# Squares and scales of weight tiles one product later, and earlier sums in the last block

## The chip, the cores and the metric

The kernel runs on one core of a Trainium2 chip. The metric is the device time of one execution in microseconds (us). The kernel before took 1020.46 us (median of three runs, 1018.66 to 1020.50); the run that the profiler recorded took 1019.09 us.

## What is computed

Four blocks follow each other on x, a matrix of 2048 tokens by 640 channels: a spectral block A, a mixer block B, then A and B again with the same weights. The change touches only the two mixer blocks.

```python
def _B_ref(x, w1, b1, w2, b2):           # x: (1, 2048, 640)
    h = _layernorm(x, axis=-1)
    u = jnp.einsum("bsd,sf->bdf", h, w1) + b1        # w1: (2048, 1728)
    u = _gelu(u)
    y = jnp.einsum("bdf,fs->bds", u, w2) + b2        # w2: (1728, 2048)
    return y.transpose(0, 2, 1)
...
x = x + _A_ref(_layernorm(x), A_w_r, A_w_i)
x = x + _B_ref(_layernorm(x), B_w1, B_b1, B_w2, B_b2)
x = x + _A_ref(_layernorm(x), A_w_r, A_w_i)
x = x + _B_ref(_layernorm(x), B_w1, B_b1, B_w2, B_b2)
```

## The kernel before

**Numbers in two halves.** TensorE (PE) multiplies float16 numbers, so each float32 operand is scaled and split into a high and a low float16 part, and a product is three matmuls: high by high, high by low, low by high. For a weight tile the parts are called `wh` and `wl`. ScalarE (ACT) makes `wh`, VectorE (DVE) makes `wl` out of the raw tile and `wh`.

**The first mixer block (`b1st`, L910).** Its weights come as 30 tiles, numbered m: 0 to 13 are columns of w1, 14 to 29 are columns of w2. Each tile has one product on PE: from m = 2 on product m is 96 matmuls of 320 columns for w1 (16 steps j of 6 matmuls, L978), and 82 for w2. Products 0 to 13 give the rows of u; product 14 is the first that reads u, in the order of its rows 0 to 13. A tile goes through these steps:

- load: `wload` (L845) reads it in two halves (c = 0 and 1) into `raw`. There are three buffers, and tile m + 3 takes that of tile m, half by half. It is asked for at the start of product m (`ahead`, L943); its DMA starts when the last reader of that half is done, and that is the making of `wl` of tile m.
- scan: `scan1` (L203) squares and sums each half on ACT (tiles `junk`, `sq`).
- scale: `scale1` (L210) has three steps, each run by one call of `step`: a reduction on DVE (`sqb`), a matmul of one column on PE with a matrix of ones, and on DVE some eight tiny operations that end in the tile's scale `s`.
- split: `wsplit` (L857) makes `wh` and `wl` of each half. Their buffers are free when the product two before has ended.
- sums: for the pairs of tiles (3, 2), (5, 4), ... (13, 12), DVE forms four sums S1 to S4 of half tiles (`wsum`, L893), which ACT and DVE split (`wssplit`, L901, tile `sp`) and GpSimd's queue (POOL) stores in DRAM for the second mixer block. S1 reads both halves of the odd tile.

After each w1 product, ACT reads it from PSUM (`t`, `q`), and ACT and DVE work out the gelu (`q`, `uf`). Once the scales of all w1 tiles are known, `scale_u` (L265) fixes one scale `su` for u, and `usplit` (L961) makes `uh` and `ul` of every row on DVE, in the order of `SEQ` (rows 6, 13, 0, 7, 1, 8, ... 5, 12). Row 12 is the last: it comes out of product 13.

**What sets the order.** The loops L989 to L1056 and L1086 to L1142 say at which step of which product each operation is written. Most of `b1st` is not pinned, so the scheduler of the framework places an engine's instructions by its own estimate of when they can start, beginning from that written order. On the chip each engine runs its list strictly in the order that comes out, and what waits holds up all behind it.

**The last block (`b2nd`, L1160).** Everything is pinned to the written order. Its second half multiplies by w2 in 56 products (n, L1600) of seven row blocks of u. The row block that is finished last (`LATE`) is left out of products 0 to 3 and added to all four together during n = 3. `hi` and `lo` (L1231, L1238) make the two parts of a weight sum three and two products ahead, `form` (L1220) makes the sums on DVE, `xbias` adds a bias to the rows of x on ACT, and `evict` (L1542) adds a finished product to x; for the first two products that takes an ACT copy `m` first.

Of the kernel before, what the change touches and what calls it, by code (L numbers as in the profile page):

```python
# [20 lines left out]
NJ, NG, NFT = 16, 16, 14  # L21
# [45 lines left out]
class Layers:  # L67
# [842 lines left out]
    def b1st(self, li):  # L910
# [78 lines left out]
        for ft in range(NFT):  # L989
# [10 lines left out]
            for j in run:  # L1000
                if ft % 2 and ft < NFT - 2 and 11 <= j < 15:
                    self.wsum(ft + 2, ("S1", "S3", "S2", "S4")[j - 11])
                if ft > 1:
                    m = ft + 1 - ft % 2
                    d = SEQ[m - 1]
                    if ft < m and j == 7:
                        q = [self.st[0][:, t:t + 1] for t in (d, d + 7)]
                        V.tensor_tensor(self.s1p[:, d:d + 1], *q, op=ALU.min)
                    if j in ((9, 14) if ft < m else (1, 7)):
                        self.wssplit(m, {9: "S1", 14: "S2", 1: "S3", 7: "S4"}[j])  # L1010
# [10 lines left out]
                else:  # L1021
                    if ft == 2 and j in (4, 5):
                        step(3)
                    if ft == 2 and j in (5, 6):
                        self.scan1(4, (j - 5,))
                    if ft == 2 and j == 7:
                        step(4)
                    if j in ((6, 8) if ft == 2 else (2, 4)):
                        next(steps)
                    if ft == 2 and j in (10, 11) or ft > 2 and j in (4, 5):  # L1030
                        step(ft + 2)
                    if j == 8 and ft == NFT - 3:
                        self.scale_u()
                    if j in (11, 13):
                        self.scan1(ft + 3, (j // 2 - 5,))
                    if j == 15:
                        step(ft + 3)
                    if ft == NFT - 2 and j % 2 or ft == NFT - 1 and j % 3 == 0 and 0 < j < 13:
# [47 lines left out]
        for j in range(NJ):  # L1086
            wh, wl = self.w.pop(NFT + j)
            ahead(NFT + j, (wh, wl))
            m = NFT + j
# [21 lines left out]
            for i, (ft, a) in enumerate(order):  # L1111
# [4 lines left out]
                if i in (4, 8):  # L1116
                    next(steps, None)
                if i in (6, 7):
                    step(m + 2)
# [40 lines left out]
    def b2nd(self, li):  # L1160
# [439 lines left out]
        for n in range(NP2 + 1):  # L1600
# [6 lines left out]
            if n == 3:  # L1607
                for k in range(4):
                    product(k, [LATE], start=False)
            if n in (2, 4):  # L1610
                xbias(n // 2 - 1)
            for k in {0: (), 1: (), 2: (), 3: (), 4: (0, 1, 2, 3)}.get(n, (n - 1,)):
                evict(k)
                q = ops[N1 + k][0]
                left[q] -= 1
                if not left[q] and q + 3 < NQ:
                    xload(q + 3)
                    extra[n + 4].append(lam(xbias, q + 3))
            if n == 5:
                xbias(2)  # L1620
            if n > 2:
                hi(N1 + n + 3)
            if n > 3:
                lo(N1 + n + 2)
# [303 lines left out]
```

## Time and profile before

| | us |
|---|---|
| median of three runs (lowest, highest) | 1020.46 (1018.66, 1020.50) |
| the profiled execution | 1019.09 |
| its span, first to last instruction | 1017.3 |
| PE busy / DVE busy / ACT busy | 968.7 / 782.9 / 577.6 |
| first mixer block, w1 products | about 210 to 372 of the span |
| first mixer block, w2 products | about 372 to 565 |
| last block, w2 products | about 853 to the end |

Times inside the span count from its first instruction. The difference of 1.8 us between the execution and its span lies outside the instructions. In the rows of a timeline stand: start, duration, engine, line of the helper that issues it (L59), operation, the tile written and those read, shape, count, and in brackets how long the engine was idle before and on what. A matmul's duration is its latency; the pace of PE is seen from start to start, 0.136 us for 320 columns.

### The profile page before, as it was taken

What the parts mean: (1) busy time and instruction counts of PE and PEld (TensorE: products, weight loads), DVE (VectorE), ACT (ScalarE), POOL (GpSimd) and SP (SyncE); (2) the same over time, 40 slices, a digit from 0 to 9 for tenths busy, and PEclk for the clock granted to TensorE, in tenths of its full rate; (3) what the DMA queues carried; (4) which work ended last, traced back from release to release, by engine and by line L of the source; (5) the groups of instructions that cost most, each with busy time, mean ns of one, the idle gap of its engine ahead of it and who ended that gap; (6) DMA issues with size and microseconds to landing.
All of it is one profiled execution on the core that took longest, in us unless ns stands there. A gap on an engine that the chain in (4) does not pass through costs nothing.

```text
span 1017.3 us, 20999 instructions
## 1 busy us (share of the span) xinstructions
PE 968.7 (95%) x8235; PEld 719.4 (71%) x8235; DVE 782.9 (77%) x1493; ACT 577.6 (57%) x890; POOL 299.9 (29%) x502
## 2 busy tenths in 40 slices
PE   3879999999999999999999799999999999999998
PEld 2768767667777767777777588776777777677776
DVE  7978968997866894666666689789965547898885
ACT  4857658687666654555553367685643434544531
POOL 6937857512211211222222278575000000000000
PEclk9599999999999999999999899999999999999999
DMA  7865346656665556465423465375444446755411
GB/s 230 278 187 163 116 157 225 218 170 247 227 215 200 189 166 247 142 189 154 135 90 111 128 183 181 93 230 173 151 160 167 166 158 222 247 183 190 152 45 53
DMA packets 67259, 176.45 MB, mean 173 GB/s; under 512 B 7996, under 2 KB 15320, under 8 KB 67160
## 3 DMA queue, kind: packets, MB, share of 16 engines
q1 hardware_dynamic: 59384, 146.92, 45.0%
q0 software_dynamic: 7776, 28.20, 7.5%
q8 instruction: 64, 1.05, 0.4%
q14 instruction: 35, 0.29, 0.1%
HBM read 127.24 MB, written 47.84 MB: 172 GB/s over the span
## 4 chain that ended last, share of the span: by engine, by line
PE 41%; DVE 27%; issue 10%; ACT 9%; POOL 7%; DMA 6%; SPq 0%; POOLq 0%; ACTq 0%; DVEq 0%
PE ps L59 41%; DVE wl L59 5%; DVE f L59 3%; DVE st L59 3%; POOL eo L59 3%; DMA xt<-x 2%; DVE s1l L59 2%; ACT wh L59 2%; DVE xt L59 2%; DVE Yl L59 2%; DMA w1S<-sp 1%; POOL xt L59 1%; ACT z L59 1%; DMA raw<-w 1%; DVE hl L59 1%
## 5 line engine op out<-in xcount | busy, mean ns | idle before, releaser
L59 PEld LDWEIGHTS <-wh 128*128 128x128 f16 x2602 | 252.4, 98 | 100.2 <-issue 2.1
L59 PEld LDWEIGHTS <-wl 128*128 128x128 f16 x1610 | 157.6, 98 | 62.8 <-issue 1.1
L59 PE MATMUL ps<-ul,wh 128*128 128x320 f16 x448 | 133.0, 299 | 0.1
L59 PE MATMUL ps<-uh,wl 128*128 128x320 f16 x448 | 133.0, 299 | 0.0
L59 PE MATMUL ps<-uh,wh 128*128 128x320 f16 x416 | 124.3, 299 | 0.0
L59 PE MATMUL ps<-hl,wh 128*128 128x320 f16 x496 | 102.9, 300 | 0.9 <-DVE hl L59 0.8
L59 PEld LDWEIGHTS <-wo 128*128 128x128 f16 x756 | 73.9, 98 | 29.7 <-DVE wo L59 1.0
L59 DVE SCALAR_TENSOR_TENSOR wl<-raw,s,wh 128x896 f16<-128x896 f32 (+2 forms) x64 | 74.5, 1168 | 12.4 <-ACT wh L59 12.2
L59 ACT ACTIVATE junk<-raw 128x896 bf16<-128x896 f32 (+1 forms) x60 | 59.5, 992 | 39.2 <-DMA raw<-w 39.0
L59 POOL TENSOR_TENSOR r<-v,mh 128x1 f32<-128x1 f32 x64 | 36.3, 567 | 151.1 <-DVE nm L59 141.2
L59 PE MATMUL ps<-tDi,Yh 128*128 128x322 f16 x320 | 72.7, 305 | 0.2
L59 DVE TENSOR_TENSOR f<-eo 128x256 f32<-128x256 f32 (+1 forms) x124 | 39.0, 367 | 38.5 <-POOL eo L59 37.9
L59 ACT ACTIVATE wh<-raw,s 128x896 f16<-128x896 f32 (+2 forms) x68 | 67.2, 1010 | 1.6 <-DVE s L59 1.6
L59 POOL TENSOR_TENSOR xt<-xt,ec 128x320 f32<-128x320 f32 x64 | 52.3, 839 | 34.9 <-DVE xt L59 34.7
L59 ACT ACTIVATE z<-xt,nb,r 128x640 f32<-128x640 f32 x31 | 28.5, 919 | 57.0 <-POOL z L59 44.5
L59 PE MATMUL ps<-ph,tS 128*128 128x321 f16 (+2 forms) x288 | 58.6, 286 | 1.3 <-DVE tb L59 1.3
L59 DVE BATCH_NORM_STATS2 st<-xt 128x6 f32<-128x320 f32 x126 | 55.2, 480 | 6.0 <-DMA xt<-x 5.0
L59 PE MATMUL ps<-u,wo 128*128 128x320 f16 x420 | 59.0, 299 | 0.7 <-DVE wo L59 0.7
L59 PE MATMUL ps<-hha,wh 128*128 128x320 f16 x288 | 58.8, 302 | 0.0
L59 POOL TENSOR_TENSOR eo<-z 128x320 f32<-128x320 f32 x62 | 53.3, 880 | 17.1 <-ACT z L59 15.1
L59 PE MATMUL ps<-tDi,Yl 128*128 128x322 f16 x192 | 56.6, 303 | 1.5 <-DVE Yl L59 1.5
L59 PE MATMUL ps<-tM,f 128*128 128x128 f32 x160 | 36.9, 395 | 21.8 <-DVE f L59 21.7
(250 smaller groups left out, 2374.1 us busy)
## 6 DMA issues: line engine op xcount, KB each, us to landing
xt<-x SPq DMA_DIRECT2D x79, 320.0 KB
raw<-w SPq DMA_DIRECT2D x32, 512.0 KB
w<-w SPq DMA_DIRECT2D x48, 321.0 KB
x<-xt SPq DMA_DIRECT2D x47, 320.0 KB
raw<-w SPq DMA_DIRECT2D x32, 448.0 KB
raw<-w2z SPq DMA_DIRECT2D x32, 448.0 KB
w1S<-sp POOLq DMA_DIRECT2D x24, 512.0 KB, 3.2
out<-xt SPq DMA_DIRECT2D x15, 320.0 KB
```

The costliest lines, as they stand in the source:

```text
L59: i = f(*a, **k)
```

## The change

In the first mixer block, for tiles 5 to 15, the scan of tile m is written in product m - 2 at steps 1 and 3 and no longer in product m - 3 at steps 11 and 13; its reduction at step 6 of product m - 2 and no longer at step 15 of product m - 3; its matmul and its tiny operations at steps 10 and 11 and no longer at 4 and 5. The splits stay where they were. Product 2 and product 14 carry tiles over by other steps, so that the places fit together; `scale_u` and the first reduction of `s1p` follow by four steps and one.

In the last block, the first four products are evicted two and two (n = 3 and 4) and no longer all at n = 4, the bias of the second row of x comes one product earlier, and `lo` of sum 6 is made at n = 3 between the two pairs of evictions.

```diff
@@ b1st, w1 products
-                    if ft < m and j == 7:
+                    if ft < m and j == 8:
...
-                    if ft == 2 and j in (4, 5):
+                    if ft == 2 and j in (6, 7):
                         step(3)
...
-                    if j in ((6, 8) if ft == 2 else (2, 4)):
+                    if j in ((9, 11) if ft == 2 else (2, 4)):
                         next(steps)
-                    if ft == 2 and j in (10, 11) or ft > 2 and j in (4, 5):
+                    if ft > 2 and j in (1, 3):
+                        self.scan1(ft + 2, (j // 2,))
+                    if j in (10, 11) or ft > 2 and j == 6:
                         step(ft + 2)
-                    if j == 8 and ft == NFT - 3:
+                    if j == 12 and ft == NFT - 3:
                         self.scale_u()
-                    if j in (11, 13):
-                        self.scan1(ft + 3, (j // 2 - 5,))
-                    if j == 15:
-                        step(ft + 3)
@@ b1st, w2 products
-                if i in (6, 7):
+                if j == 0 and i in (1, 3):
+                    self.scan1(m + 2, (i // 2,))
+                if i in ((8, 12, 13) if j == 0 else (6, 7)):
                     step(m + 2)
@@ b2nd
-            if n in (2, 4):
-                xbias(n // 2 - 1)
-            for k in {0: (), 1: (), 2: (), 3: (), 4: (0, 1, 2, 3)}.get(n, (n - 1,)):
+            if n in (2, 3):
+                xbias(n - 2)
+            for k in {0: (), 1: (), 2: (), 3: (0, 1), 4: (2, 3)}.get(n, (n - 1,)):
                 evict(k)
...
-            if n > 3:
+            if n == 3:
+                lo(N1 + 6)
+            if n > 4:
                 lo(N1 + n + 2)
```

What the scheduler makes of it shows in the lists of the engines. DVE, around the reduction `sqb` of tile 15, before: it stands behind the splits of u's rows 6, 13, 0, 7, 1, 8 and 2.

```order
L59 SCALAR_TENSOR_TENSOR ul2_546_3346<-uf2_547_3363,su_130,uh2_546_3332 128x640
L59 TENSOR_SCALAR s1_73<-qi1_732_5108 128x1
L59 SCALAR_TENSOR_TENSOR sp_735_5186<-S2_720_5021,sp1_79,sp_735_5186 128x1024
L59 TENSOR_SCALAR s1_73<-s1_73 128x1
L59 TENSOR_REDUCE sqb1_737_5197<-sq_734_5161 128x1
L59 TENSOR_SCALAR uh9_546_3339<-uf9_547_3370,su_130 128x640
```

And now (`qt` is the squared sum of tile 13, `uf4` the gelu of product 10, `qm` the first operation of `scale_u`):

```order
L59 SCALAR_TENSOR_TENSOR uf4_547_3365<-q_704_4886,t_703_4885 128x640
L59 TENSOR_SCALAR qt_76<-ps714_4978 128x1
L59 TENSOR_REDUCE sqb1_745_5267<-sq_743_5227 128x1
L59 TENSOR_SCALAR qi1_716_4989<-qt_76 128x1
L59 TENSOR_REDUCE qm_5003<-qt_76 128x1
```

The reduction has moved 39 instructions up: ahead of `scale_u` and of every split of u.

ACT, between the splits of tiles 10 and 11, before (`junk_69,sq_702` is the scan of tile 13, `sp` the splits of S1, S2 and S3 of the pair 11, `wh_697` the split of tile 11, `t` and `q` the reading of product 9):

```order
L59 ACTIVATE junk_69,sq_702_4851<-raw_695_4757 128x1024
L59 ACTIVATE sp_701_4835<-S1_686_4706,sp1_79 128x1024
L59 ACTIVATE sp_703_4872<-S2_689_4724,sp1_79 128x1024
L59 ACTIVATE junk_69,sq_702_4851<-raw_696_4759 128x1024
L59 ACTIVATE sp_712_4912<-S3_688_4716,sp1_79 128x1024
L59 ACTIVATE wh_697_4765<-raw_665_4470,s0_72 128x1024
```

And now, the same operations:

```order
L59 ACTIVATE junk_69,sq_711_4911<-raw_693_4752 128x1024
L59 ACTIVATE junk_69,sq_711_4911<-raw_694_4754 128x1024
L59 ACTIVATE sp_699_4826<-S1_685_4699,sp1_79 128x1024
L59 ACTIVATE sp_702_4869<-S2_688_4722,sp1_79 128x1024
L59 ACTIVATE wh_695_4760<-raw_663_4465,s0_72 128x1024
L59 ACTIVATE t_690_4744<-ps675_4605,b1s_67,c0_74 128x640
```

Both halves of the scan of tile 13 still stand ahead of the split of tile 11, now also ahead of S1 and S2; S3 has gone behind the split. Between the splits of tiles 9 and 10 the list of ACT is as before: scan of tile 12, then the split of tile 10.

DVE in the last block, both kernels (`xt` is an eviction, `wo0_1566` and `wo0_1568` are `lo` of sum 6, `wo1_1571` that of sum 7, S1 to S4 are formed sums):

```order
 L59 TENSOR_TENSOR S1_1565_12010<-raw_1554_11933,raw_1555_11935 128x896
-L59 TENSOR_TENSOR S2_1567_12044<-S1_1565_12010,raw_1556_11937 128x896
 L59 SCALAR_TENSOR_TENSOR xt_1552_11927<-ps1563_11952,c1_75,xt_1552_11927 128x320
 L59 SCALAR_TENSOR_TENSOR xt_1553_11930<-ps1563_11952,c1_75,xt_1553_11930 128x320
+L59 SCALAR_TENSOR_TENSOR wo0_1568_12050<-S1_1565_12010,sp_77,wo0_1568_12050 128x896
+L59 TENSOR_TENSOR S2_1569_12053<-S1_1565_12010,raw_1556_11937 128x896
 L59 SCALAR_TENSOR_TENSOR xt_1552_11927<-ps1564_11989,c1_75,xt_1552_11927 128x320
 L59 SCALAR_TENSOR_TENSOR xt_1553_11930<-ps1564_11989,c1_75,xt_1553_11930 128x320
-L59 SCALAR_TENSOR_TENSOR wo0_1566_12042<-S1_1565_12010,sp_77,wo0_1566_12042 128x896
 L59 TENSOR_TENSOR S3_1572_12081<-raw_1556_11937,raw_1554_11933 128x896
```

`lo` of sum 6 now stands ahead of the second sum and of the last two evictions; `lo` of sum 7 follows eight operations after S1, as before.

## The prediction

> **What bounds the kernel now.** I read the page first, then PE's waits in the first mixer block, then the timelines around the longest.
>
> ```profile
> span 1017.3 us, 20999 instructions
> PE 968.7 (95%) x8235; PEld 719.4 (71%) x8235; DVE 782.9 (77%) x1493; ACT 577.6 (57%) x890; POOL 299.9 (29%) x502
> PE ps L59 <- DVE sqb L59: 2.9, 2, 2.3
> PE ps L59 <- DVE wl L59: 0.2, 1, 0.2
> ```
>
> PE is busy for 95%, and in the w1 products it waits for almost nothing but the squared sums, 2.9 us in two places. The longer one is that of tile 15, in product 13:
>
> ```profile
> 357.77 0.43 PE L59 MATMUL ps<-hha,wl 128*128 128x320 f16 x2
> 360.52 0.16 PE L59 MATMUL ps<-sqb,ones 128*128 128x1 bf16 x1 [2.32 <-DVE sqb L59]
> ```
>
> The one-column matmul starts 2.75 us after the pair at 357.77, which takes 0.27, so 2.5 us are lost. Behind it comes a stretch at half clock, which the busy times by windows show (its columns: stretch, length, then busy time and count of PE, PEld, DVE, ACT and POOL, then the granted clock):
>
> ```profile
> 361.30:364.70 3.40, 3.40 (x15) 1.95 (x14) 3.40 (x7) 2.11 (x4) 1.44 (x1) 0.52 0.42 166
> ```
>
> 3.4 us at a clock of 0.52 are 1.7 us more. So the wait is worth 4.2 us to PE. But PE has another wait behind it, in product 14, which reads u:
>
> ```profile
> 381.81 0.30 PE L59 MATMUL ps<-uh,wh 128*128 128x320 f16 x1
> 382.24 0.30 PE L59 MATMUL ps<-ul,wh 128*128 128x320 f16 x1
> ```
>
> 0.43 from start to start, 0.30 too long: here PE waits for `ul` of row 12, the last to be split. So this end is set by DVE, by 0.3 us, and not by the wait of 4.2. What DVE did from the last scale of w1 on:
>
> ```profile
> 343.07 0.15 DVE L59 TENSOR_SCALAR qt<-ps 128x1 f32<-128x1 f32 x1
> 343.25 0.15 DVE L59 TENSOR_SCALAR qi<-qt 128x1 int32<-128x1 int32 x1
> 347.44 1.00 DVE L59 TENSOR_SCALAR uh<-uf,su 128x640 f16<-128x640 f32 x2
> ...
> 360.24 0.14 DVE L59 TENSOR_REDUCE sqb<-sq 128x1 bf16<-128x2 f32 x1
> 374.40 0.14 DVE L59 TENSOR_SCALAR qi<-s 128x1 int32<-128x1 int32 x1
> 381.30 0.88 DVE L59 SCALAR_TENSOR_TENSOR ul<-uf,su,uh 128x640 f16<-128x640 f32 x1
> ```
>
> And the windows of the same stretch:
>
> ```profile
> 343.00:349.50 6.50, 6.50 (x51) 4.67 (x50) 6.40 (x25) 4.32 (x7) 1.97 (x2) 1.00 0.62 206
> 349.50:358.00 8.50, 8.50 (x65) 6.05 (x62) 8.50 (x12) 5.24 (x6) 1.66 (x3) 1.00 0.42 147
> 358.00:375.00 17.00, 14.68 (x98) 9.97 (x97) 16.76 (x35) 9.20 (x13) 2.82 (x6) 0.90 0.57 190
> ```
>
> DVE, the third busy number, works 31.7 of 32 us. The block's turn from w1 to w2 is a DVE queue without holes, from 343.25 to `ul` of row 12 at 382.18.
>
> **The change, part 1: the new wait.** The scan of tile 15 needs tile 15 loaded:
>
> ```profile
> 339.86 2.91 SPq L851 DMA_DIRECT2D raw<-w  x2
> 344.12 0.95 ACT L59 ACTIVATE junk<-raw 128x896 bf16<-128x896 f32 x1 [2.39 <-DMA raw<-w]
> 348.30 0.95 ACT L59 ACTIVATE junk<-raw 128x896 bf16<-128x896 f32 x1 [1.06 <-DMA raw<-w]
> 375.18 1.03 ACT L59 ACTIVATE wh<-raw,s 128x896 f16<-128x896 f32 x1
> ```
>
> Its halves are asked for as `wl` of tile 12 frees its buffers, at 339.86 and 342.44 (2.91 for both issues, of which each takes 0.33), and the second lands at 348.30, 8.4 us after the first was asked for. The scan ends 1.1 later, at 349.4. Before, the reduction stood far down DVE's list and ran at 360.24: the load cost nothing. Now it stands right behind `qt` of tile 13, ahead of `scale_u` and all splits of u, and DVE's list is strict: DVE stops at about 343 and waits for the load. Behind it stand the same 31.1 us of DVE work (343.25 to 374.40, the scale of tile 15), and behind that the last chain on ACT and DVE: `wh` of tile 15, reading product 13, gelu, split of row 12 (375.18 to 382.18, 7.0 us). So row 12 is ready at B + 38.1, B being the start of DVE's block, 343.25 before (with 0.8 of slack, since ACT waited for another load).
>
> **Where B falls.** It is 9.5 us after the first half of `wl` of tile 12, which before ended at 339.8. Whether this comes earlier is a matter of a loop: `wl` of tile m frees the buffer, the load of tile m + 3 follows, its scan stands in ACT's list ahead of the split of tile m + 1.
>
> ```profile
> 257.22 1.28 DVE L59 SCALAR_TENSOR_TENSOR wl<-raw,s,wh 128x1024 f16<-128x1024 f32 x1 [0.41 <-ACT wh L59]
> 272.42 1.28 DVE L59 SCALAR_TENSOR_TENSOR wl<-raw,s,wh 128x1024 f16<-128x1024 f32 x1
> 285.36 1.28 DVE L59 SCALAR_TENSOR_TENSOR wl<-raw,s,wh 128x1024 f16<-128x1024 f32 x1 [0.88 <-ACT wh L59]
> 295.03 1.06 ACT L59 ACTIVATE junk<-raw 128x1024 bf16<-128x1024 f32 x1 [0.78 <-DMA raw<-w]
> 300.21 1.28 DVE L59 SCALAR_TENSOR_TENSOR wl<-raw,s,wh 128x1024 f16<-128x1024 f32 x1
> 310.11 1.06 ACT L59 ACTIVATE junk<-raw 128x1024 bf16<-128x1024 f32 x1 [3.10 <-DMA raw<-w]
> 312.33 1.28 DVE L59 SCALAR_TENSOR_TENSOR wl<-raw,s,wh 128x1024 f16<-128x1024 f32 x1 [0.88 <-ACT wh L59]
> 327.85 1.28 DVE L59 SCALAR_TENSOR_TENSOR wl<-raw,s,wh 128x1024 f16<-128x1024 f32 x1
> 338.55 1.28 DVE L59 SCALAR_TENSOR_TENSOR wl<-raw,s,wh 128x1024 f16<-128x1024 f32 x1 [0.89 <-ACT wh L59]
> ```
>
> These are the first halves of tiles 6 to 12, with the second scans of tiles 11 and 12. From tile 7 to 9 are 27.8 us, from 9 to 11 27.6; two products on PE are 192 x 0.136 = 26.1. So the loop is slower than PE, and the splits fall behind.
>
> An odd leg now: the second half of the load lands 8.4 after `wl` (295.03 - 286.64). Then scan 1.05, S1's split on ACT 1.05, four DVE operations (S1, S2, two new sums) at 1.2, `wl` 1.3: 16.6 us, where before 14.9 (tile 9) and 15.5 (tile 11) were enough, because the S1 and S2 splits ran during the load. An even leg: the second half of `wl` follows the first by 2.0 and not by 3.1, as no sum stands between; the load lands some 7.7 after, not 8.6; the rest stays at 3.5 (310.11 to 313.61): 11.1, where before 12.1. So a pair takes 27.7 as before, and only the start helps:
>
> ```profile
> 230.31 1.15 ACT L59 ACTIVATE sp<-S,sp 128x1024 f16<-128x1024 f32 x1 [2.82 <-DMA w1S<-sp]
> 239.76 1.15 ACT L59 ACTIVATE sp<-S,sp 128x1024 f16<-128x1024 f32 x1 [3.52 <-issue]
> ```
>
> These two waits shrink, since S1 of pair 3 is now split one `wl` (1.2 us) earlier and S1 of pair 5 no longer stands behind a scan. I take 2.8 us of lead at tile 6 (255.7 for the end of `wl`), as an estimate from these rows: less 4.6 on the three odd legs 7, 9, 11, plus 3.6 on the even ones 8, 10, 12, gives a lead of **1.8 us** at tile 12. Its ends are -1 (the loads land no earlier on the even legs) and 4 (the odd legs cost nothing more). B is then 338.0 + 9.5 = 347.6 and row 12 is split at 385.7, 3.5 us later than before; by the ends of the lead, 1.4 to 6.4.
>
> In those sums the load counts with the 5.9 us that the row shows for the second half (342.44 to 348.30). The Trainium skill's page "DMA: Bandwidth & Descriptors", section "Anatomy of one DMA", has about 2.0 us plus the bytes at 436 GB/s; for 448 KB that is an estimate of 3.1 us. By that rule B would be 2.8 earlier and the loss 0.7 and not 3.5; the row differs, and it decides.
>
> **What goes.** The wait of tile 15's matmul goes: it now stands 36 matmuls (4.9 us) later, and its reduction runs at 347.6, ahead of its place at about 362. So do the 0.2 at `wl` of tile 11. Both lie ahead of row 12 and are given back waiting for it. The wait of tile 3, 0.54 us in the list of waits, stays: its matmul moves by one place, and the three sums ahead of its reduction remain. Tile 16's sum is needed long after it is there. Product 15's tile and all later loads had over 5 us to spare, and PE does not wait from there to 557; so what is lost at row 12 shows in the end.
>
> **Part 2, the last block.**
>
> ```profile
> 871.44 1.80 PE L59 MATMUL ps<-u,wo 128*128 128x320 f16 x12 [0.71 <-DVE wo L59]
> 867.71 0.55 DVE L59 SCALAR_TENSOR_TENSOR xt<-ps,c,xt 128x320 f32<-128x320 f32 x1 [1.89 <-ACT m L59]
> 870.24 1.14 DVE L59 SCALAR_TENSOR_TENSOR wo<-S,sp,wo 128x896 f16<-128x896 f32 x1
> 872.76 1.14 DVE L59 SCALAR_TENSOR_TENSOR wo<-S,sp,wo 128x896 f16<-128x896 f32 x1
> ```
>
> PE loses 0.9 us (1.01 from start to start) for `lo` of sum 6, ready at 871.38. Now it comes after two evictions and no longer after four and a sum: about 869.6, and the wait goes. But `lo` of sum 7, at 873.9 before, still has eight operations after S1 ahead of it, DVE waits no less for `m`, and it comes at 874.1. PE, now 0.9 earlier, needs it at 873.4 and gets it at about the time at which it used it before (874.3). So 0.0, between -0.9 (sum 7 is in time) and +0.4 (the lag of 0.2 to 0.4 shows at a later sum).
>
> **The sum.** 1019.09 + 3.5 + 0.0 = 1022.6 on the profiled execution. That execution lies 1.4 below the median of 1020.46, and 3.5 on the median is 1024.0; I take 1023.4, between the two.
>
> **The rivals.** *Faster (the intended way):* the odd legs do not lengthen, and the loop follows PE. The deciding point is a lead of 5.3 us at tile 12, `wl` before 334.5; then row 12 is ready before 382.2. At best PE gains all that it lost: 4.2 + 0.3 at row 12 + 0.2 at tile 11 + 0.9 = 5.6, which is 1014.9 on the median. For it: ACT no longer stands in two halves around the sums. Against it: every scan stands ahead of a split and behind a load, as before. With the clock, the rows show half pace after an idle stretch of 2.3 us; the Trainium skill's "TensorE: Matmul & The Clock Gate", section "What's actually happening", has it after an idle window of about 3.4 us, by which 2.5 and not 4.2 would go at tile 15. The row speaks against that; the limit would be 1016.6.
>
> *No change:* tile 15's second half lands faster, as that of tile 16 does:
>
> ```profile
> 354.97 2.72 SPq L851 DMA_DIRECT2D raw<-w  x2
> 361.18 0.95 ACT L59 ACTIVATE junk<-raw 128x896 bf16<-128x896 f32 x1 [1.80 <-DMA raw<-w]
> ```
>
> Its issue begins at 357.36, and it lands 3.8 later, not 5.9. Then B is 345.5 and the loss 1.4; on the median, 1021.9.
>
> *Slower still:* the loads gain nothing on even legs, a lead of -1, and PE, which waits for rows 4 and 5 as well, runs at half clock behind them: 3.5 + 2.8 + about 1 = 7.3, 1027 between the execution and the median.
>
> **How the numbers follow.** The forecast's mechanism 0.72 (its own range 1020.8 to 1026.5), faster 0.13, no change 0.10, slower still 0.05. About 0.2% (2 us) is what a measurement of this kernel can tell from no change. A fifth of the forecast's own weight lies within it, so: faster 0.14, same 0.20, slower 0.66. The range 1018.8 to 1026.8 leaves out the faster cases and the far end of the slow ones.
>
> **What would show it.** Right: a new DVE wait of 3 to 7 us ahead of `sqb`, ended by ACT's `junk`, at about 343 to 348; no PE wait for `sqb` in product 13; PE waiting for `ul` of rows 4, 5 and 12, the last at about 385.7; `wl` of tile 12 at 336 to 340; in the last block the wait for `wo` moved by one sum. Wrong: `wl` of tile 12 before 334.5, or DVE without that hole.

## The result and the profile after

The changed kernel takes 1028.05 us (median of four runs, 1027.96 to 1030.97), the kernel before, on the same chip, 1020.48 (1018.66 to 1021.68). The ratio is 1.0083 with a 95% interval of 1.0059 to 1.0106: slower by 7.6 us between the medians, more than twice what was forecast and beyond the range. The profiled execution took 1027.96 us.

First the page, its span and busy times; then the list of PE's waits, with the five rows that concern the two mixer blocks (us in all, times, longest):

```profile
span 1026.2 us, 20994 instructions
PE 972.6 (95%) x8235; PEld 722.0 (70%) x8235; DVE 781.7 (76%) x1493; ACT 577.8 (56%) x890; POOL 299.4 (29%) x502
```

```profile
PE ps L59 <- DVE wl L59: 4.4, 4, 2.6
PE ps L59 <- DVE uh L59: 2.6, 1, 2.6
PE ps L59 <- DVE ul L59: 1.5, 2, 1.0
PE ps L59 <- DVE wo L59: 0.4, 1, 0.4
PE ps L59 <- DVE sqb L59: 0.4, 1, 0.4
```

The span is 8.9 us longer. The wait for the squared sums has shrunk from 2.9 us to 0.4, and in its place PE now waits 4.4 for `wl`, the low halves of w1, and 4.1 for the rows of u.

Set against before, operation by operation, after runs 0.3 us ahead at 200 us of the span, 8.16 late at 394, 8.22 at the first mixer block's end, and 8.88 at the end. Of this, 8.5 us arise in the first mixer block, 0.6 in the spectral block behind it, and 0.07 in the last block.

DVE's timeline at the turn from w1 to w2:

```profile
347.03 0.15 DVE L59 TENSOR_SCALAR qt<-ps 128x1 f32<-128x1 f32 x1
352.33 0.16 DVE L59 TENSOR_REDUCE sqb<-sq 128x1 bf16<-128x2 f32 x1 [5.15 <-ACT junk L59]
353.54 0.54 DVE L59 TENSOR_SCALAR uh<-uf,su 128x640 f16<-128x640 f32 x1
...
389.64 0.88 DVE L59 SCALAR_TENSOR_TENSOR ul<-uf,su,uh 128x640 f16<-128x640 f32 x1
```

The new hole stands in the second row: DVE stops for 5.15 us, and the splits of u begin behind it. The last row is the low half of row 12, done at 390.52 and not at 382.18: 8.34 us later, about as much as the block loses.

The hole alone is not 8.3 us. `qt` of tile 13, the last operation ahead of it, already runs 3.96 us later than before (347.03 against 343.07): the loop over the w1 tiles had slowed down before it. A leg of this loop is the time from the end of the first half of `wl` of one tile to that of the next, called odd or even by the second tile's number. These are the first halves of tile 6 and, six legs later, of tile 12:

```profile
256.22 1.28 DVE L59 SCALAR_TENSOR_TENSOR wl<-raw,s,wh 128x1024 f16<-128x1024 f32 x1 [0.89 <-ACT wh L59]
342.51 1.28 DVE L59 SCALAR_TENSOR_TENSOR wl<-raw,s,wh 128x1024 f16<-128x1024 f32 x1 [0.89 <-DMA w1S<-sp]
```

The one ends at 257.50, 1.0 us earlier than before, the other at 343.79, 4.0 us later. Two legs between them, first on DVE (the odd leg of tile 7, then the even leg of tile 8):

```profile
268.18 0.16 DVE L59 TENSOR_REDUCE sqb<-sq 128x1 bf16<-128x2 f32 x1 [6.91 <-ACT junk L59]
269.86 2.48 DVE L59 SCALAR_TENSOR_TENSOR sp<-S,sp,sp 128x1024 f16<-128x1024 f32 x2 [1.09 <-ACT sp L59]
274.65 1.28 DVE L59 SCALAR_TENSOR_TENSOR wl<-raw,s,wh 128x1024 f16<-128x1024 f32 x1
...
285.65 0.16 DVE L59 TENSOR_REDUCE sqb<-sq 128x1 bf16<-128x2 f32 x1 [2.26 <-ACT junk L59]
287.32 1.28 DVE L59 SCALAR_TENSOR_TENSOR wl<-raw,s,wh 128x1024 f16<-128x1024 f32 x1 [0.89 <-ACT wh L59]
```

then the same two on ACT:

```profile
267.00 1.06 ACT L59 ACTIVATE junk<-raw 128x1024 bf16<-128x1024 f32 x1 [2.99 <-DMA raw<-w]
268.68 2.19 ACT L59 ACTIVATE sp<-S,sp 128x1024 f16<-128x1024 f32 x2 [0.54 <-DVE sp L59]
...
284.46 1.06 ACT L59 ACTIVATE junk<-raw 128x1024 bf16<-128x1024 f32 x1 [1.96 <-DMA raw<-w]
286.13 1.15 ACT L59 ACTIVATE wh<-raw,s 128x1024 f16<-128x1024 f32 x1 [0.52 <-issue]
```

Read them together: the scan of a tile that is just landing ends on ACT (at 268.06 and 285.52), then its reduction runs on DVE (`sqb`), then those tiny operations that end in the scale of the tile two before, the one that is split next: they now stand behind that reduction, and only when they are done can ACT go on, with `wh` or with the splits of S1 and S2, whose scale is made of the same numbers. ACT's idle 0.54 and 0.52 us behind the scans are this detour over DVE. (The first of these rows names `sp` on DVE: the scale of the sums, `sp1`, is printed like their splits. For the second the profile names no releaser; the scale that `wh` reads is written between 285.90 and 286.05, and `wh` starts at 286.13.)

What PE sees of it, in its timeline:

```profile
302.06 0.43 PE L59 MATMUL ps<-hl,wh 128*128 128x320 f16 x2
305.05 0.45 PE L59 MATMUL ps<-hha,wl 128*128 128x320 f16 x2 [2.55 <-DVE wl L59]
...
379.92 0.30 PE L59 MATMUL ps<-uh,wh 128*128 128x320 f16 x1 [2.62 <-DVE uh L59]
381.18 0.43 PE L59 MATMUL ps<-ul,wh 128*128 128x320 f16 x1 [0.96 <-DVE ul L59]
383.48 0.43 PE L59 MATMUL ps<-ul,wh 128*128 128x320 f16 x1 [0.49 <-DVE ul L59]
...
882.84 0.85 PE L59 MATMUL ps<-u,wo 128*128 128x320 f16 x5 [0.45 <-DVE wo L59]
```

and the window behind the three waits for u (stretch, length, busy time and count of PE, PEld, DVE, ACT, POOL, then the clock):

```profile
381.30:387.70 6.40, 5.91 (x23) 3.12 (x22) 5.15 (x14) 4.13 (x5) 0.00 (x0) 0.50 0.29 102
```

The late `wl` halves and the late rows 4 and 5 of u make PE wait, and it then runs at a clock of 0.50 for 6.4 us; from start to start of its matmuls, the half pace costs 4.2 us in this block (1.6 behind the 2.55, 2.6 behind the rows of u), 1.6 before. PE comes to row 12 at 391.25, 0.7 us after that is ready, and does not wait for it.

### The profile page after: what moved, and what is told of

Its sections match the earlier page's. It is cut to its first block, busy times and chain, and to the rows that moved or that the text cites. A ratio compares the mean times of both kernels' runs of the same rounds, so it can differ in the third digit from the quotient of the medians.

```text
span 1026.2 us, 20994 instructions
## 1 busy us (share of the span) xinstructions
PE 972.6 (95%) x8235; PEld 722.0 (70%) x8235; DVE 781.7 (76%) x1493; ACT 577.8 (56%) x890; POOL 299.4 (29%) x502
## 4 chain that ended last, share of the span: by engine, by line
PE 35%; DVE 16%; ACT 7%; DMA 5%; issue 3%; POOL 3%; SPq 0%; ACTq 0%; DVEq 0%; POOLq 0%
PE ps L59 35%; DVE wl L59 4%; DMA xt<-x 3%; DVE st L59 2%; ACT wh L59 2%; POOL eo L59 2%; DVE xt L59 2%; ACT z L59 1%; DVE f L59 1%; DMA raw<-w 1%; DVE s1l L59 1%; ACT junk L59 1%; DVE ul L59 1%; ACT xt L59 1%; DMA raw<-w2z 1%
## 5 line engine op out<-in xcount | busy, mean ns | idle before, releaser
L59 PE MATMUL ps<-hha,wl 128*128 128x320 f16 x256 | 53.9, 302 | 3.7 <-DVE wl L59 3.7
```

The lines of the kernel that those rows point to most:

```text
L59: i = f(*a, **k)
```

## The experiments

The theory to begin with: part 1 carries the loss, by two terms. One is the new wait at tile 15's reduction. The other is the loop of the odd and even legs, where an operation that waits for a load stands ahead of what a tile already loaded needs. The rivals: part 2; the place of tile 15's reduction alone; the order on ACT alone; and, later, another carrier from row 12 to the end of the block. Each kernel was timed in five rounds against the kernel before. `self.after(i)` in the edits queues what follows behind instruction i on its engine; it sets an order and adds no wait. Shorter words stand for its arguments: `S1_S2_split`, `tiny_ops`, `ul_row`, `last_scan`, `reduction`.

### Which part

Part 1 alone (`b1st` of the change, `b2nd` of before) and part 2 alone:

> The edit of the first mixer block alone, the last block as before. Theory (the loss arises in the w1 products, the last block adds under 0.1): 1028.0, between 1027.4 and 1028.6, with the block's end 8.4 us later than before, as with the whole change. Rival (the two parts share the loss, for instance because the later stores of the first block disturb the last one): under 1026.

> The edit of the last block alone. Theory: 1020.5 plus or minus 0.5; PE's wait for wo moves from sum 6 to sum 7 and shrinks from 0.7 to 0.4 us. Rival (sum 7 is in time when the loop is not late): 1019.6, 0.9 less.

Part 1 took 1029.51 against 1019.88, a ratio of 1.0092 (1.0075 to 1.0109); part 2 1019.49, 0.9999 (0.9987 to 1.0010). So part 1 is all of it. The single profiles of this block scatter: that of part 2 alone ran 1.2 us ahead at its end, though nothing was changed there, and that of part 1 alone ended it 11.7 us later than before, where the change, with the same code there, ended it 8.5 later. Below, verdicts go by the medians, and places in one profile are to be read with 1 to 3 us of scatter.

### The wait of tile 15 alone

The change, with tile 15's reduction held until the split of row 2 (`SEQ[6]`), where it stood before; the expectation calls this row 9:

```diff
-                    if j in (10, 11) or ft > 2 and j == 6:
+                    if ft == NFT - 1 and j == 6:
+                        with self.after(ul_row[SEQ[6]]):
+                            step(ft + 2)
+                    elif j in (10, 11) or ft > 2 and j == 6:
                         step(ft + 2)
```

> The whole change, but the reduction of tile 15 is held on DVE behind the split of u's row 9, so that the hole of 5.1 us ahead of it goes; nothing else moves. Theory (row 12 is late because DVE's block starts late, by that hole and by the late loop): DVE's block starts at 347.1; ACT still has the scan of tile 15 ahead of the split of tile 13, so DVE stops there for 1.7 us, and 3.5 of the 5.1 us come back: 1024.5, between 1023 and 1025.5. Rival (PE's own waits for wl of tiles 9, 11, 13 and 14 set the loss, and row 12 only follows): 1027 to 1028.

It took 1026.37, 1.0065 (1.0042 to 1.0088): about 2 of 8 us come back, less than expected, and its interval overlaps the change's. The rows of DVE and of PE say what took the place of the hole:

```profile
358.75 1.28 DVE L59 SCALAR_TENSOR_TENSOR wl<-raw,s,wh 128x1024 f16<-128x1024 f32 x1 [1.90 <-ACT wh L59]
```

```profile
372.34 0.18 PE L59 MATMUL ps<-sqb,ones 128*128 128x1 bf16 x1 [3.13 <-DVE sqb L59]
```

The hole of 5.15 is gone, but DVE now stops for 1.90 us at the split of tile 13, which the hole had covered, and PE waits 3.13 us for the squared sum. Row 12 came at 390.25, as late as in the change; but in this profile the loop itself was later, with `qt` of tile 13 at 349.87 and not at 347.03, so that its row 12 does not tell what the hole is worth.

The opposite, the kernel before with only tile 15's reduction put ahead of `scale_u`:

```diff
-                    if j == 8 and ft == NFT - 3:
-                        self.scale_u()
-                    if j in (11, 13):
+                    if j == 0 and ft == NFT - 2:
+                        self.scan1(NFT + 1)
+                        step(NFT + 1)
+                        with self.after(reduction):
+                            self.scale_u()
+                    if j in (11, 13) and ft != NFT - 2:
                         self.scan1(ft + 3, (j // 2 - 5,))
-                    if j == 15:
+                    if j == 15 and ft != NFT - 2:
                         step(ft + 3)
```

> The kernel before, but the scan and the reduction of tile 15 are written ahead of scale_u, so that DVE waits there for the load of tile 15; the other tiles stay as before, so the loop of loads keeps its pace. While DVE waits it has two splits of sums (2.5 us) ready, which the scheduler moves ahead of the reduction. Theory (the hole alone delays DVE's block and with it row 12): block at 349.4 and not 343.3, less the 2.5, less a slack of 0.8: 2.8 us later, 1023 where the kernel before has 1020.2; PE no longer waits for sqb in product 13. Rival (the hole alone costs nothing, only the loop does): 1020.

It took 1021.70 against 1019.07, 1.0021 (1.0005 to 1.0036). In DVE's timeline the reduction now follows the splits of the last pair's sums; DVE waits 1.52 us ahead of those and not at all ahead of the reduction:

```profile
348.50 2.48 DVE L59 SCALAR_TENSOR_TENSOR sp<-S,sp,sp 128x1024 f16<-128x1024 f32 x2 [1.52 <-ACT sp L59]
350.90 0.15 DVE L59 TENSOR_REDUCE sqb<-sq 128x1 bf16<-128x2 f32 x1
```

PE no longer waits for tile 15's sum, but it has a new wait of 4.36 us for that of tile 16, in product 14, so the 2.6 us are not DVE's wait alone. From both sides, the place of this reduction is worth about 2 to 2.6 us, by intervals 3 to 5 us wide: a quarter to a third of the loss. The rest must come from the loop.

### The order on ACT alone

The kernel before, with the splits of S1 and S2 behind the scan as in the change, and the scans and reductions where they were:

```diff
-                    if j in ((9, 14) if ft < m else (1, 7)):
+                    if ft < m and j == 14 and ft > 2:
+                        with self.after(last_scan):
+                            self.wssplit(m, "S1")
+                            self.wssplit(m, "S2")
+                    elif ft == 2 and j in (9, 14) or ft == m and j in (1, 7):
...
```

> The kernel before, but on ACT the splits of S1 and S2 are held behind the second half of the odd tile's scan, the order that the change brings about; reductions, matmuls and tile 15 as before. Theory (this order is most of the loop's loss): odd legs 16.5 to 17.5 and not 15.2, wl of tile 12 ends at 343 to 346 and not at 339.8, row 12 as much later: 1023 to 1026 where the kernel before has 1019.5, and PE waits for wl of tiles 9 or 11. Rival (the order on ACT costs nothing; the reductions on DVE do): 1020.

It took 1021.57 against 1020.28, 1.0010 (0.9995 to 1.0026), far less than expected. Its odd legs were 16.99, 15.68 and 16.59 us, its even legs 10.92, 9.70 and 10.41; against before, odd legs are 1.2 longer and even legs 1.6 shorter on average. That is the trade that the prediction worked out for the whole change (16.6 and 11.1). It is real, it is about neutral (2.7 us at most, by the interval), and it is not the loss by itself: the theory that ACT's order alone carries most of it fell here.

### The reductions and the scans held back

In the change, the reductions of tiles 5 to 14 were queued behind the scale of the tile before, so that no scale waits for the load of a later tile:

```diff
-                    if j in (10, 11) or ft > 2 and j == 6:
+                    if ft > 2 and j == 6:
+                        with self.after(tiny_ops):            # not tile 15
+                            step(ft + 2)
+                    if j in (10, 11):
                         step(ft + 2)
```

> The whole change, but for tiles 5 to 14 the reduction is held on DVE behind the scale of the tile before it; the scans on ACT stay as in the change. Theory (the reduction that waits for a scan holds up the scale that stands behind it, 0.5 to 0.6 us on each leg of the loop): six legs give 3.0 to 3.6 us, wl of tile 12 ends at 340.5 and not at 343.8, row 12 at 387: 1025, where the whole change has 1028. The rest of the loop's loss, the splits of S1 and S2 behind the second half of the scan, stays. Rival (the loads set the pace alone): 1028. Rival (the reduction's place is all of the loss): 1020 or less.

It took 1026.49, 1.0063 (1.0042 to 1.0084): 2 us came back, not 3, again with an interval that overlaps the change's. What follows the load in a leg shrank as expected, from 8.93 to 8.29 us on odd legs and from 4.1 to 3.56 on even ones. But the loads of the even legs took 8.0 us and not 7.2, and PE got a new wait, at tile 5:

```profile
PE ps L59 <- DVE sqb L59: 4.4, 2, 4.0
```

Then only the second half scan of each odd tile (and of tile 15) was queued behind the splits of S1 and S2 on ACT, with the reductions written as in the change:

```diff
-                    if ft > 2 and j in (1, 3):
-                        self.scan1(ft + 2, (j // 2,))
+                    if ft > 2 and j == 1:
+                        self.scan1(ft + 2, (0,))
+                    if ft > 2 and j == 3:
+                        with self.after(*([S1_S2_split] if ft % 2 else [])):
+                            self.scan1(ft + 2, (1,))
```

> The whole change, with one hold alone: on ACT the second half of each odd tile's scan, tile 15's included, behind the splits of S1 and S2; the scheduler places the reductions. Theory (the scan's place is most of it, and a scan behind the split takes its reduction with it): odd legs about 13, 1014 to 1018, as in the runs that hold the reductions too. Rival (the reductions have to be held as well): 1021 or more.

1014.83, 0.9950 (0.9930 to 0.9970): one held instruction per pair turns the change from 0.8% slower to 0.5% faster. It took the reductions along, as the theory has it: that of tile 9 now runs at 281.31, behind the splits of S1 and S2, with no scale waiting behind it, and that of tile 15 at 363.61, far behind `scale_u`, so that the hole is gone as well. Odd legs are 13.2 us on average, in a profile that at 1018.92 is the slowest of the seven executions, and PE's remaining long wait for squared sums is at tile 5:

```profile
PE ps L59 <- DVE sqb L59: 3.8, 2, 3.4
```

Both held, for tiles 5 to 14 and without tile 15:

```diff
+                        with self.after(S1_S2_split):          # odd tiles
+                            self.scan1(ft + 2, (1,))
...
+                        with self.after(tiny_ops, S1_S2_split):
+                            step(ft + 2)
```

> The whole change, but for tiles 5 to 14 the reduction is held on DVE behind the scale of the tile before it (for odd tiles also behind the splits of S1 and S2), and on ACT the second half of an odd tile's scan behind S1 and S2. The reduction of tile 15 stays ahead of the splits of u. Theory (the loop of load, scan and split sets the rate): an odd leg falls from 17.6 to about 12 us, an even one from 10.6 to about 11, the loop becomes faster than PE, PE no longer waits for wl, wl of tile 12 ends at 334 to 338 and not at 343.8; the hole ahead of tile 15's reduction stays, row 12 is ready at 376 to 382: 1015.5 to 1020. Rival (the loads themselves are late, whatever stands in the lists): 1026 to 1028.

1017.35 against 1019.88, 0.9975 (0.9961 to 0.9989). ACT's timeline around the split of tile 11:

```profile
313.79 2.17 ACT L59 ACTIVATE sp<-S,sp 128x1024 f16<-128x1024 f32 x2
316.22 1.15 ACT L59 ACTIVATE wh<-raw,s 128x1024 f16<-128x1024 f32 x1 [0.26 <-PE ps L59]
...
322.45 1.04 ACT L59 ACTIVATE junk<-raw 128x1024 bf16<-128x1024 f32 x1
```

The second half scan of tile 13 has gone behind the split of tile 11; ACT waits for no load there, `wh` waits for its free buffer, that is for PE. Odd legs are 13.06, 12.61 and 13.15, even ones 12.12, 10.57 and 10.72; `wl` of tile 12 ends at 331.75, below the 334.5 that the prediction gave as the point from which the loop follows PE, and row 12 is ready at 378.34. The wait ahead of tile 15's reduction is left, 2.17 us. (Later expectations call this kernel the fourth run, and the next one the eighth.)

With tile 15's scan held too and its reduction behind the split of row 13, the hole goes as well:

```diff
+                    if ft == NFT - 1:
+                        hold = [ul_row[SEQ[1]]]
```

> The fourth run (order held), and also the reduction of tile 15 held behind the split of u's row 13, so that no hole of 2.2 us is left on DVE ahead of scale_u. Theory: in the fourth run PE waits for nothing in these products, so the hole is covered: 1017.3, within 0.2% of the fourth run. Rival (row 12 still bounds there): 1 to 2 us less.

1014.34, 0.9942 (0.9924 to 0.9961): expected was no difference from the kernel ahead of it, since PE hardly waits in either. Since this miss could have been scatter, both were run again on one chip:

> The fourth run again, beside the eighth on one chip. If the hole of 2.2 us on DVE ahead of scale_u is covered, as the fourth run's trace has it, the two agree within 0.2%; if row 12 still bounds in part of the executions, this one is 2 to 3 us longer, as their first medians (1017.35 and 1014.34) have it.

> The eighth run again, beside the fourth: 1014 to 1017, faster than the kernel before by 0.3 to 0.6%.

1017.49 (0.9976, 0.9961 to 0.9991) and 1013.93 (0.9930, 0.9911 to 0.9949): the difference stands, 3.6 us. On DVE, the first of them, with the hole, the split of row 12 and the first eviction of a w2 product:

```profile
342.72 0.16 DVE L59 TENSOR_REDUCE sqb<-sq 128x1 bf16<-128x2 f32 x1 [3.27 <-ACT junk L59]
379.04 0.88 DVE L59 SCALAR_TENSOR_TENSOR ul<-uf,su,uh 128x640 f16<-128x640 f32 x1
392.41 0.88 DVE L59 SCALAR_TENSOR_TENSOR xt<-ps,c,xt 128x640 f32<-128x640 f32 x1 [5.70 <-ACT xt L59]
```

and the second, without the hole:

```profile
375.47 0.88 DVE L59 SCALAR_TENSOR_TENSOR ul<-uf,su,uh 128x640 f16<-128x640 f32 x1
388.78 0.88 DVE L59 SCALAR_TENSOR_TENSOR xt<-ps,c,xt 128x640 f32<-128x640 f32 x1 [4.42 <-ACT xt L59]
```

Row 12 moves by 3.57, the first eviction by 3.63. As a mark behind the block serves the first matmul of the next spectral block that reads `flt`. It moves with them, by 3.60; these are its rows in the one and in the other:

```profile
569.18 0.31 PE L59 MATMUL ps<-tM,flt 128*128 128x128 f16 x1
```

```profile
565.58 0.31 PE L59 MATMUL ps<-tM,flt 128*128 128x128 f16 x1
```

PE itself falls back by only 1.7 us from ahead of this block (0.46 ahead at 191) to behind row 12 (1.25 behind at 400); the rest comes in the w2 products and behind them. So something other than PE's waits up to row 12 carries DVE's delay to the end of the block.

The held order was tried on the kernel before as well, by writing the second half scan of odd tiles and its reduction one product later, behind the split of S3:

> The kernel before, but the second half of an odd tile's scan and its reduction are written one product later, behind the split of S3, so that on ACT no scan stands between the load and the split of an odd tile; nothing else of the change. Theory: the loop becomes faster than PE (odd legs 13, even 12), the block of DVE starts earlier, row 12 no longer bounds; but the matmul of the squared sum keeps its place at the 24th of 96 matmuls, and PE waits there up to 3 us where the reduction comes late: 1016 to 1021. Rival (it is the later place of the matmul alone that makes the order of the fourth run good): 1022 to 1026, with waits for sqb in several products.

It took 1032.25, 1.0119 (1.0100 to 1.0137), and says nothing on the theory. The scheduler put the reading of a product and the split of S3 ahead of the splits of odd tiles, so the order that was wanted did not come out; odd legs were 17.4 to 19.7 us, and PE waited 10.0 us for squared sums in three places.

### What carries row 12's delay to the end

From the end of row 12's split to that mark it is 188.6 to 189.7 us in all the kernels above, before and after included (189.01 and 188.89), whatever PE waits for in between. In the kernel before, SyncE's queue at that place:

```profile
377.42 2.88 SPq L851 DMA_DIRECT2D raw<-w  x2
380.82 2.67 SPq L298 DMA_DIRECT2D tM<-tM  x4
384.62 3.21 SPq L1076 DMA_DIRECT2D xt<-x  x3
```

and what hangs on it, first on ACT (the bias), then on DVE (the first eviction):

```profile
393.59 2.42 ACT L59 ACTIVATE xt<-xt,b2s 128x640 f32<-128x640 f32 x3 [7.23 <-DMA xt<-x]
```

```profile
394.45 0.88 DVE L59 SCALAR_TENSOR_TENSOR xt<-ps,c,xt 128x640 f32<-128x640 f32 x1 [5.71 <-ACT xt L59]
```

The load of tile 18 waits for `wl` of tile 15 to free its buffer. In the same queue, behind it, stand the tables of the next spectral block and then the rows of x to which the w2 products are added. So a late DVE makes x late, DVE stops 5.7 us for it, and the evictions follow at 12.14 us each, about the 12.0 that a product takes. In the change:

```profile
392.96 3.62 SPq L1074 DMA_DIRECT2D xt<-x  x3
```

```profile
401.75 2.42 ACT L59 ACTIVATE xt<-xt,b2s 128x640 f32<-128x640 f32 x3 [7.06 <-DMA xt<-x]
```

the bias comes 8.16 later, about the block's loss. To test this chain, x was made later (the four `tM` tables loaded twice ahead of it) in the kernel before:

```diff
         self.a0_load()
+        for q in range(4):
+            self.a0_load_m(q)
```

> The kernel before, but the four tables tM are loaded a second time ahead of the first rows of x. Nothing ahead of the end of product 13 changes, row 12 is split at about 382, PE meets it as before. Theory (the load of x, the first eviction and the pace of the evictions set the end): the load lands 4 to 9 us later, the end of the block as much later, 1024 to 1029. Rival (row 12 sets it through PE): 1020.

1020.46 against 1020.16, 1.0012 (0.9997 to 1.0027). The bias moved by 3.0 us, but the third eviction by only 1.2 and the mark by 1.3: the delay was smaller than expected, and the evictions caught up most of it. Then x was loaded ahead of the tables, in the kernel before, in the change, and in the held version:

```diff
-        for q in range(4):
-            self.a0_load_m(q)
-        self.a0_load()
...
         xts = [load(0), load(1)]
+        for q in range(4):
+            self.a0_load_m(q)
+        self.a0_load()
```

> The kernel before, but the first two rows of x are loaded ahead of the tables tM, tS and tI. Theory: the first eviction comes 4 to 7 us earlier, the evictions no longer set the end, and PE does: 0.9 us that its last squared sum is late against its own pace of 12.0, and 1.4 less from there to the end, so 2.3 us: 1018. Rival (row 12 through PE): 1020.3, no change.

> The whole change with the first two rows of x ahead of the tables. PE's products behind row 12 run at their own pace of 12.0 us there already, so PE takes over at once: 1.4 us at the end, 1027. Rival (the x load alone carries the loss): 1020.

> The order held for all tiles (eighth run) with the first two rows of x ahead of the tables. Its products run at their own pace throughout, 40.0 us from the last squared sum to the end and not 41.3, so the two limits already meet: 1013 to 1014, up to 1 us less.

Before: 1017.66, 0.9978 (0.9964 to 0.9991). The queue and the bias:

```profile
381.76 0.91 SPq L1073 DMA_DIRECT2D xt<-x  x2
382.72 2.14 SPq L298 DMA_DIRECT2D tM<-tM  x4
```

```profile
387.45 0.83 ACT L59 ACTIVATE xt<-xt,b2s 128x640 f32<-128x640 f32 x1 [2.02 <-DMA xt<-x]
```

x is read 6.1 us earlier, and from row 12's split to the mark it is 186.72 us and no longer 189.0: 2.3 us were the x chain's, then PE is the limit. The starts of the products say the same: in the kernel before they follow each other at 12.00 us until 445 and at 12.13 from 457 on, the pace of the evictions; with x early they stay at 12.00. In the change the products follow each other at 12.00 us even with x late. With x early it took 1027.72, 1.0082 (1.0057 to 1.0106), no better than without, although its chain is 186.72 too. PE's waits there:

```profile
PE ps L59 <- DVE wl L59: 5.9, 3, 3.3
PE ps L59 <- DVE uh L59: 3.2, 2, 2.6
PE ps L59 <- DVE ul L59: 1.5, 2, 1.0
```

So the rival that the load of x alone carries the loss (1020 by it) falls: with x early, the late halves of w1 and rows of u carry all of it through PE. Two limits lie within 2.3 us of each other, and both start from DVE. The held version with x first took 1015.30, 0.9953 (0.9933 to 0.9973), no better than the held version alone, although its profiled block was 7.2 us shorter than before's. There the mark stands 189.05 us behind row 12's split, although the first eviction came 8.2 us earlier than in the held version alone (380.62 against 388.78): with row 12 and x both early, PE's own pace sets the end, and the distance from row 12 no longer says anything. The held version alone has the lowest medians, 1013.93 and 1014.34, and beats both kernels; the kernel with one scan held (1014.83) cannot be told from it.

## Why the prediction was wrong, point by point

**What bounds the kernel: right as far as it went.** The end of the block was said to be set by DVE through row 12 and not by PE's longest wait. Row 12 moved by 8.34 us and the mark behind the block by 8.22. Not as forecast was that PE would wait for row 12 itself: held up by rows 4 and 5 and the half clock behind them, it came there 0.7 us after row 12 was ready.

**The new wait: right.** It was forecast ahead of `sqb` of tile 15, ended by ACT's `junk`, 3 to 7 us long; it is 5.15. From B, now 352.33, the sum gave row 12 at B + 38.1 = 390.4; it was ready at 390.52.

**Where B falls: this step failed.** It gave a lead of 1.8 us for `wl` of tile 12; it came 4.0 us later than before (343.79 against 339.83), beyond the worse end of -1. B is 4.7 us later than the 347.6 forecast, and row 12 with it: 385.7 against 390.5. By terms:

| term | forecast | measured | adds to B, us |
|---|---|---|---|
| `wl` of tile 6, first half, ends | 255.7 | 257.50 | +1.8 |
| six legs from there, as put down | 82.3 | (83.4 by its own terms) | +1.1 |
| odd legs, load | 8.4 | 8.55 (mean) | +0.4 |
| odd legs, rest | 8.2 | 8.93 (each) | +2.2 |
| even legs, load | 7.7 | 7.18 (mean) | -1.6 |
| even legs, rest | 3.5 | 4.10 (mean) | +1.8 |
| from `wl` of tile 12 to B | 9.5 | 8.54 | -1.0 |

The legs add for three of each kind; the terms give +4.7, as B does. The second row is a slip of arithmetic: three pairs of 27.7 are 83.1 (83.4, since 7.7 and 3.5 are 11.2 and not 11.1), but the legs were reckoned as 4.6 lost and 3.6 won, which leaves 82.3. The main row is the rest of the legs, +4.0 together: what follows the landing of the load in a leg was taken as too short. The prediction counted on odd legs the scan, the split of S1 and four DVE operations, and left even legs at 3.5.

It overlooked that the reduction of a tile just landing now also stands on DVE ahead of the tiny operations that end in the scale of the tile to be split next. The prediction looked for that only at tile 15, where the order of the lists was shown; it stood in every leg. In all four profiles whose loop is the change's (the change, part 1 alone, tile 15 held, the change with x first) this rest is 8.93 to 8.95 us on odd legs and 4.02 to 4.14 on even ones, while the loads differ (7.27 to 9.86 and 6.50 to 8.84); in the five with the loop of before the rest is 6.37 to 7.39 and 3.40 to 3.51. So the rest is the change's doing, and the row of the loads is in part scatter. Holding the reductions took the rests back to 8.29 and 3.56, as this reading wants. That the estimate of the legs was sound for ACT's order alone, the kernel with that order shows (16.4 and 10.3 on average).

The lead of 2.8 at tile 6 was the other mis-sized term; it was 1.0: `wl` of tile 5 came 3.7 earlier (244.91 against 248.58), but the leg from there to tile 6 took 12.6 us against 9.9.

**The load: between the bounds.** Tile 15's second half was asked for at 346.40 and landed at 351.25: 4.85 us, where 5.9 was taken and 3.8 was the rival's. By the Trainium skill's page "DMA: Bandwidth & Descriptors", section "Anatomy of one DMA", it would be an estimate of 3.1; the page gives its fit for transfers that GpSimd issues, this load is issued by SyncE, and this trace differs here too.

**What goes: right, but incomplete.** PE's wait for tile 15's sum is gone, and what was saved was given back at row 12, as said. Not said was that `wl` of tiles 9, 11, 13 and 14 would be late (4.4 us of PE's waits, 2.55 at tile 9). The sentence that all later loads had over 5 us to spare overlooked the rows of x: they stand in the queue behind the load of tile 18, and DVE's first eviction waited 5.71 us for them in the kernel before. The conclusion, that what is lost at row 12 shows in the end, held, for two reasons instead of one.

**Part 2: right.** 0.0 was forecast; 0.07 us was seen in the trace, and a ratio of 0.9999 alone. The wait for `wo` moved from 871.44 to 882.84; less the 8.88 of the shift this is 873.96, the place of sum 7, as forecast, with 0.45 us in place of 0.71.

**The rivals.** *Slower still* saw what came: PE waiting for rows 4 and 5 (2.62, 0.96 and 0.49) and half clock behind it. But its sum was not: these waits lie beside the time that row 12 takes anyhow, and the 8.3 us are all B. *Faster* gave 1014.9 as the limit where the loop follows PE: the held version reached 1013.93 and 1014.34, so the limit was about right; and with the order held and the hole left, `wl` of tile 12 ended at 331.75, ahead of the 334.5, and row 12 at 378.34, ahead of the 382.2, as its condition has it. The change missed it by the order of one scan in each pair, and of the reductions that go with it. By the Trainium skill's page "TensorE: Matmul & The Clock Gate", section "What's actually happening", half clock follows an idle window of about 3.4 us; here it followed a wait of 2.55, and one of 2.62 with short ones behind it, so the trace again speaks for less.

**The chance.** The failed step had been given ends of -1 and 4 from two of its own terms, the even loads and the odd legs, and none from the start or from what else might stand in a leg. All four uncertain terms of a loop that runs six times should have widened it. The chances at the end do not follow from the weights either: 0.10 and a fifth of 0.72 make 0.24 for no change and leave 0.63 for slower.

**What stays open.** The single parts, as far as they could be tried alone, are the place of tile 15's reduction (2 to 2.6 us), the reductions in the loop (2 us, by holding them) and ACT's order (1 us); they sum to 5 or 6 of 8, and each of them is about as large as its interval is wide. With the reductions of the loop held, the hole of tile 15 (4.92 us there) and ACT's order are left, and 6.4 us of loss (1.0063), more than the 3 or 4 that these two cost one by one. Holding one scan of each pair, on the other hand, is worth some 13 us (0.9950 against 1.0083), more than the loss; but that moves the odd tiles' reductions and that of tile 15 as well. What is shown is that the order around the landing loads carries the loss, not how much each part of it does. The parts are not additive: in a loop around a buffer each leg starts from the one before, and the landing of the loads (9.50, 7.46 and 8.68 us on odd legs of the same kernel) is a part of it that no run here took apart. A run with smaller loads, which would have told, was not tried.

## What to carry to other kernels

When a step is moved to a different place in a strict list, look in every turn of the loop, on each engine that the step touches, for what now stands directly behind the instruction that waits for a load: a small one (here a reduction of 0.16 us, ahead of which DVE stood for 5.15 us) can cost far more than its own time, since all behind it takes over its wait. A loop that runs around a buffer is worth an order set by hand: here one scan per pair, held behind work that has its data already, was worth more than the whole change lost, with the reductions that moved along. And before saying that what follows has time to spare, follow each transfer queue as well as each engine: here a load that waited for a buffer until 377.42 held up the tables and the rows of x behind it, which have nothing to do with it.

## What the runs showed of the hardware that was not expected

Short waits were enough to halve PE's pace here: after 2.62, 0.96 and 0.49 us of waiting within 4 us, the granted clock was 0.50 for 6.4 us, at a cost of 2.6 us from start to start of the matmuls, on top of the 4.1 us of the waits themselves. After the single wait of 2.55 us in product 9 the half pace cost 1.6 us.

The landing of one and the same load is uneven: the second half of tile 15 landed 5.86 us after its request in the kernel before, 4.85 in the change, and 6.2 with ACT's order alone, with the same bytes on the same queue, one profile each. And the rows of x, 9.0 us from their issue (384.62) to the bias in the kernel before, took 5.7 when they stood ahead of the tables, and 5.9 when they stood behind twice as many of them: the number of tables ahead of them does not by itself tell how long they take. What does, no run here shows.
